# The last group of layer 2: a plain weight quadrant for the left-over block, its rows stored per two batches, and casts and sums in another order

## The chip, the cores and the metric

One core of one Trainium2 chip runs one launch of the kernel. The metric is the device time of that launch in microseconds (us). TensorE does the matrix products, VectorE (DVE) the element-wise work on two operands, ScalarE (ACT) casts, copies and activations, and SyncE (SP) issues most of the transfers; each engine takes its own instructions strictly in program order and waits on semaphores for the others. Transfers issued by SP and by ACT run on 16 shared DMA engines.

## What is computed

The reference is linear attention over 4 batches of 576 rows, followed by two feed-forward layers; only the second layer is touched:

```python
x = attention(q, k, v, omega)            # [4 * 576, 512]
r = np.maximum(x @ moe_w_in, 0.0);  x = (r * r) @ moe_w_out
h = x @ moe2_w_in                        # 512 -> 2048
g = np.where(h > 0.0, h, np.exp(np.minimum(h, 0.0)) - 1.0)
out = (g @ moe2_w_out).astype(np.float32)   # 2048 -> 512
```

## The kernel before

**Precision.** Every float32 operand is split into a high part (a cast on ACT, names ending in `h`) and a low part (a subtraction on DVE, recorded at line 77, names ending in `l`). A product is the sum of three matmuls: high by high, high by low, low by high.

**Tours.** The 2048 hidden columns of a layer are taken in four groups of 512. Within a group the rows come in five tours: four full ones (512 rows of one batch each, i = 0 to 3) and a left-over one, "block B", which holds the last 64 rows of all four batches (256 rows). In the last group of layer 2, written `(1, NG - 1)`, block B is the last tour of the kernel.

**Products by quadrants.** In the groups of the list `SECOND`, to which the last group of layer 2 belongs, both matrix products of a full tour use seven block products in place of eight. Each is 12 matmuls of 256 columns. In the first matrix product the seven operands of x are called b, t3, t2, p, t1, t4, q; they are read back from DRAM by SP (line 729), always five operands ahead of use in program order. In the second the hidden blocks "11", "12", "21", "22" and their differences t1 to t4 meet weight quadrants "A", "B", "C", "D" (function `strassen`, line 837). "A" is the pair of plain quadrants of the even weight slices; "B" holds the first plain quadrant of the odd slices beside the SUM of two second quadrants, since `make_floats` overwrites `b2` (line 172). The seven products are `p1` to `p7` in `quadrants`; they run one tour late, woven by `toured` (`earlier(0)` to `earlier(3)`) between the products of the next tour. Their results stand in PSUM banks x, r, y, z, v: bank y is copied by ACT to z in `p6` (line 880) and to v in `p7` (line 888), and p4 goes on in v. `grown` (line 921) adds a bank to the output rows in SBUF, in instructions of 256 columns on DVE, and in the last group at once calls `stored`, which issues the transfer to DRAM.

**Activation of layer 2.** `squares` gives three ACT instructions (relu, exp, tanh; four with a copy for block "12"), `joined` two on DVE (lines 951, 952), `difference` one on DVE (line 957), and `halved` a cast on ACT (line 963) and a subtraction on DVE.

**Order.** All of it is emitted in a hand-written order (`tc.manual_schedule()`): the place of a call in `toured` is its place in the queue of its engine. The list `carried` runs in the next tour after its first two products, `behind` after `earlier(0)` and `earlier(1)`, `sums` wherever `run(sums)` stands. Weight casts and their low parts are "chores", dealt out by `slot`.

**The left-over block** uses four products, in the order x += A by 11, x += B by 21 (`e0`), r += B by 21, r += A by d, with d = 11 - 21 (`e1`). Its output of 128 rows (two batches by 64) and 256 columns is stored by two transfers of 64 rows, one from SP and one from ACT (line 975); there are eight of these.

Of the kernel before, what the change touches and what calls it, by code (L numbers as in the profile page):

```python
# [17 lines left out]
def linear_attention_two_ffn_kernel(  # L18
# [12 lines left out]
    nc = tc.nc  # L31
# [115 lines left out]
    def make_floats(n):  # L147
        p = parts[n]
        t, m = staged.pop(p)
        nc.vector.scalar_tensor_tensor(  # L150
            out=t, in0=m.bitcast(U32), scalar=3, in1=t, op0=ALU.logical_shift_left, op1=ALU.bitwise_or
        )
        staged[p] = t.bitcast(F32)
        moe, f, o = p
        if not summed_up(p):
            return
        tf_t[f] = staged[p]
        names = "ABCD" if o else "abcd"
        if f % 2 == 0:
            casts.append(((moe, f, names[0]), tf_t[f]))  # L160
            return
        a, b = tf_t.pop(f - 1), tf_t.pop(f)
        sub = page([W], f"cs{moe}_{f}_{o}")
        if f % GF == 1:
            combos[f // GF] = page([W], f"cd{moe}_{f}_{o}")
        d = combos[f // GF][:, f % GF // 2 * HN:(f % GF // 2 + 1) * HN]
        (a1, a2), (b1, b2) = ((t[:, :HN], t[:, HN:]) for t in (a, b))
        s2, s3 = sub[:, :HN], sub[:, HN:]
        tt = nc.vector.tensor_tensor
        if o:  # L170
            tt(out=s3, in0=b1, in1=b2, op=ALU.subtract)
            tt(out=b2, in0=a2, in1=b2, op=ALU.add)
            tt(out=s2, in0=b2, in1=b1, op=ALU.subtract)
            tt(out=d, in0=a1, in1=s2, op=ALU.subtract)
        else:
            tt(out=s3, in0=a1, in1=b1, op=ALU.subtract)
            tt(out=b1, in0=b1, in1=b2, op=ALU.add)
            tt(out=s2, in0=b1, in1=a1, op=ALU.subtract)
            tt(out=d, in0=a2, in1=s2, op=ALU.subtract)
        casts.append(((moe, f - 1, names[1]), b))  # L180
        casts.append(((moe, f - 1, names[2]), sub))
        if f % GF == GF - 1:
            casts.append(((moe, f // GF * GF, names[3]), combos.pop(f // GF)))
# [642 lines left out]
    def strassen(tour, y, name, half, key, fresh):  # L826

        moe, g, k, i = tour
        gh, gl = g2_t[tour, key]
        for pr in range(2):  # L830
            wh, wl = ws_t[moe, g * GF + (0 if name == "D" else 2 * pr), name]
            c0 = pr * HN if name == "D" else half * HN
            for e in range(2):
                cs = slice(c0 + e * P, c0 + (e + 1) * P)
                ts = slice(pr * HN + e * P, pr * HN + (e + 1) * P)
                for m, (a, w) in enumerate(((gh, wh), (gh, wl), (gl, wh))):
                    nc.tensor.matmul(
                        y[:, e * HN:(e + 1) * HN],
                        *((a[:, ts], w[:, c0:c0 + HN]) if moe else (w[:, cs], a[:, pr * HN:(pr + 1) * HN])),
                        start=fresh and pr == 0 and e == 0 and m == 0, stop=pr == 1 and m == 2, skip_group_check=True,  # L840
                    )
# [7 lines left out]
    def quadrants(tour):  # L849

        moe, g, k, i = tour
        if moe == 0:
            sown(4, moe, g)
        elif k == 0 and (moe, g - 1) not in SECOND:
            del seeds[2:]
        nm = f"{moe}_{g}_{i}"
        bank = dict(zip("yzv", seeds[1:]))

        def part(to, name, half, key, fresh=False):
            if fresh:  # L860
                bank[to] = psum(f"p{to}{nm}")
            strassen(tour, bank[to], name, half, key, fresh)

        def add(to, l, u, last=True):
            sums.append(lambda: grown(tour, bank[to], l, u, last))

        def p1():
            part("x", "B", 0, "22", True)
            nc.scalar.copy(out=bank["y"], in_=bank["x"])

        def p5():
            part("r", "B", 1, "t1", True)
            add("r", 0, 0, False)
            add("r", 0, 1, False)

        def p6():
            part("y", "C", 0, "t2")
            sown(4, moe, g)
            bank.update(zip("zv", seeds[2:]))
            nc.scalar.copy(out=bank["z"], in_=bank["y"])  # L880

        def p2():
            part("x", "A", 0, "12")
            add("x", 1, 0)

        def p7():
            part("y", "C", 1, "t3")
            nc.scalar.copy(out=bank["v"], in_=bank["y"])
            add("y", 0, 1)

        def p3():
            part("z", "D", 0, "11")
            add("z", 0, 0)

        def p4():
            part("v", "A", 1, "t4")
            add("v", 1, 1)
            ended(tour)

        def e0():  # L900
            part("x", "A", 0, "11", True)
            part("x", "B", 0, "21")
            add("x", 0, 0)

        def e1():
            part("r", "B", 1, "21", True)
            part("r", "A", 1, "d")
            add("r", 0, 1)
            ended(tour)

        if i == B:
            return [[e0], [], [e1], []]
        return [[p1], [p5, p6], [p2, p7], [p3, p4]] if moe else [[p1, p5], [p6, p2], [p7, p3], [p4]]

    def grown(tour, y, l, u, last):
        moe, g, k, i = tour
# [50 lines left out]
    def stored(i, t, ya, cs):  # L967
        if i < B:
            (nc.scalar if (i, t) == (B - 1, 3) else nc.sync).dma_start(
                out=out[i * S:i * S + C * P, cs].rearrange("(p c) e -> p c e", c=C)[:, t, :], in_=ya[:, cs]  # L970
            )
            return
        for v in range(P // L):
            bb = t * (P // L) + v
            (nc.scalar if v else nc.sync).dma_start(out=out[bb * S + C * P:(bb + 1) * S, cs], in_=ya[v * L:(v + 1) * L, cs])

    def summed(tour, l):
        moe, g, k, i = tour
# [38 lines left out]
    def toured(before):  # L1017
# [3 lines left out]
        for n, tour in enumerate(tours):  # L1021
# [10 lines left out]
            if i == B:  # L1032
                bank_e, bank_o = psum(f"pe{nm}"), psum(f"po{nm}")
                times(tour, bank_e, "a", 0, "u", True, False, True)
                times(tour, bank_e, "a", 1, "v", False, True, False)
                read(tour, "v")
                run(carried)
                chores = chores_of(tour)
                slot(chores, 2)
                earlier(0)  # L1040
                carry(0)
                act = squares if second else act_a
                act(tour, "11", bank_e)
                times(tour, bank_o, "b", 0, "u", True, False, True)
                times(tour, bank_o, "b", 1, "d", False, True, False)
                read(tour, "d")
                earlier(1)
                carry(1)
                act(tour, "21", bank_o)
                joined()  # L1050
                if second:
                    halved(tour, "11")
                else:
                    act_b(tour, "11")
                run(sums)
                earlier(2)
                if second:
                    halved(tour, "21")
                    difference(tour, "d", "11", "21")
                    halved(tour, "d")  # L1060
                else:
                    act_b(tour, "21")
                slot(chores, 1)
                earlier(3)
                run(sums)
                if second:
                    todo = quadrants(tour)
                else:
                    todo = [[lambda tour=tour: chunk(tour, "11", True, False)], [], [lambda tour=tour: chunk(tour, "21", False, True)], []]
                continue  # L1070
# [30 lines left out]
            product(w, "b", 1, "t4")  # L1101
            nc.vector.tensor_tensor(out=c21, in0=w, in1=us, op=ALU.add)
            run(sums)
            act(tour, "22", c22)
            joined()
            slot(chores, 2)
            earlier(2)
            act(tour, "21", c21)
            joined()
            if second:  # L1110
                halved(tour, "22")
            else:
                act_b(tour, "22")
            product(b, "d", 0, "q")
            act(tour, "12", b)
            if second:
                run(sums)
                difference(tour, "t1", "21", "22")
                difference(tour, "t2", "11", "t1")
                halved(tour, "t1")  # L1120
                difference(tour, "t3", "11", "21", "21")
                joined()
            else:
                act_b(tour, "21")
            slot(chores, 1)
            earlier(3)
            run(sums)
            if second:
                carried.append(lambda tour=tour: halved(tour, "t2"))
                carried.append(lambda tour=tour: halved(tour, "12"))  # L1130
# [118 lines left out]
```

## Time and profile before

| | us |
|---|---|
| median of 3 runs (907.88 to 908.86) | 908.32 |
| the profiled execution, its own time | 908.27 |
| its span | 906.5 |
| PE busy | 894.5 |
| DVE busy | 711.2 |
| ACT busy | 607.7 |

The span runs from the first to the last instruction of the profile; 1.77 us of the execution's time lie outside it. PE is the matmul row; its instructions overlap, so that a stall is read from the distance of two starts, not from the busy share. The granted clock is at its full level in all 40 slices of the page.

### The profile page before, as it was taken

The numbers are of one execution on the slowest core, as the hardware profiler recorded it, in microseconds if no ns is written. First come the engines' busy times: TensorE is split into PE (matmuls) and PEld (weight loads), VectorE is DVE, ScalarE is ACT, GpSimd is POOL, SyncE is SP. The second block draws the span as 40 slices with busy tenths as digits, with TensorE's granted clock in tenths as the row PEclk, the third lists the DMA queues.
The fourth block names the chain that finished last, engine by engine and source line by source line (L and its number), as shares of the span: only waits on it lengthen the run. The fifth ranks groups of instructions, "written<-read, shape, count | busy, mean of one in ns | idle before, by whom it ended". The sixth has DMA issues, their size and how long they took to land. (4 is left out here: it accounts for less than half of the span.)

```text
span 906.5 us, 20710 instructions
## 1 busy us (share of the span) xinstructions
PE 894.5 (99%) x7807; PEld 844.4 (93%) x7807; DVE 711.2 (78%) x1329; ACT 607.7 (67%) x1292; POOL 86.8 (10%) x188
## 2 busy tenths in 40 slices
PE   8999999999999999999999999999999999999997
PEld 7888999998999999999999999899899989989997
DVE  5898875688876888777879897966597748878887
ACT  7999976664767675766366666755485638666663
POOL 4678730000000000000000000000000000000000
PEclk9999999999999999999999999999999999999999
DMA  9675522524998676577589664275468655653653
GB/s 242 168 196 159 170 83 75 177 94 154 349 374 302 216 250 239 179 231 255 197 279 335 244 209 164 96 256 195 160 203 270 222 183 168 205 200 126 222 173 94
DMA packets 134724, 183.89 MB, mean 203 GB/s; under 512 B 34272, under 2 KB 70624, under 8 KB 134624
## 3 DMA queue, kind: packets, MB, share of 16 engines
q1 hardware_dynamic: 133328, 181.88, 60.3%
q8 instruction: 62, 1.02, 0.5%
q10 hardware_dynamic: 1296, 0.69, 0.3%
q14 instruction: 38, 0.31, 0.1%
HBM read 145.29 MB, written 37.22 MB: 201 GB/s over the span
## 5 line engine op out<-in xcount | busy, mean ns | idle before, releaser
L810 PE MATMUL py<-wh,gh 128*128 128x512 f32 x216 | 85.2, 394 | 0.0
L810 PE MATMUL py<-wl,gh 128*128 128x512 f32 x216 | 85.1, 394 | 0.0
L810 PE MATMUL py<-wh,gl 128*128 128x512 f32 x216 | 85.1, 394 | 0.0
L782 DVE SCALAR_TENSOR_TENSOR r<-r,t 128x512 f32<-128x512 f32 x54 | 37.1, 687 | 57.4 <-ACT t L781 57.4
L77 DVE TENSOR_TENSOR gl<-gf,gh 128x512 fp32r<-128x512 f32 (+1 forms) x104 | 65.0, 625 | 4.1 <-ACT gh L792 0.5
L810 PEld LDWEIGHTS py<-wh,gl 128*128 128x128 f32 x216 | 40.6, 188 | 9.6
L810 PEld LDWEIGHTS py<-wl,gh 128*128 128x128 f32 x216 | 40.6, 188 | 7.4
L810 PEld LDWEIGHTS py<-wh,gh 128*128 128x128 f32 x216 | 40.6, 188 | 7.4
L135 ACT ACTIVATE cm<-st 128x512 f32<-128x512 f32 x64 | 44.2, 698 | 2.1 <-DMA st<-in_moe_w_out_dram 1.8
L792 ACT CAST gh<-gf 128x512 fp32r<-128x512 f32 x54 | 33.3, 617 | 17.0 <-DVE gf L783 16.1
L150 DVE SCALAR_TENSOR_TENSOR cv<-cm,cv 128x512 uint32<-128x512 uint32 x64 | 43.4, 685 | 0.8
L1082 ACT COPY pb<-pa 128x512 f32<-128x512 f32 x28 | 16.1, 574 | 40.1 <-PE pa L759 39.9
L1097 DVE TENSOR_TENSOR c<-pb,vs 128x512 f32<-128x512 f32 x28 | 19.3, 690 | 28.3 <-PE pb L759 21.7
L818 PE MATMUL py<-gh,wh 128*128 128x256 f32 x144 | 40.4, 281 | 0.0
L818 PE MATMUL py<-gh,wl 128*128 128x256 f32 x144 | 40.4, 281 | 0.0
L818 PE MATMUL py<-gl,wh 128*128 128x256 f32 x144 | 40.4, 281 | 0.0
L1090 ACT COPY us<-pb 128x512 f32<-128x512 f32 x28 | 16.4, 587 | 34.6 <-PE pb L759 29.1
L549 PE MATMUL ph<-xh,wh 128*128 128x256 f32 (+1 forms) x128 | 38.8, 303 | 0.0
L585 PE MATMUL py<-gh,wh 128*128 128x256 f32 (+1 forms) x128 | 38.4, 300 | 0.0
L585 PE MATMUL py<-gl,wh 128*128 128x256 f32 (+1 forms) x128 | 37.8, 295 | 0.0
L585 PE MATMUL py<-gh,wl 128*128 128x256 f32 (+1 forms) x128 | 37.8, 295 | 0.0
L549 PE MATMUL ph<-xh,wl 128*128 128x256 f32 (+1 forms) x128 | 37.7, 295 | 0.0
(1250 smaller groups left out, 3608.7 us busy)
## 6 DMA issues: line engine op xcount, KB each, us to landing
st<-in_moe_w_in_dram SPq DMA_DIRECT2D x32, 512.0 KB, 5.4
st<-in_moe_w_out_dram SPq DMA_DIRECT2D x32, 512.0 KB, 3.8
vk<-in_v_dram SPq DMA_DIRECT2D x32, 128.0 KB, 4.7
out_dram<-ya SPq DMA_DIRECT2D x30, 128.0 KB, 2.0
ld0k<-in_k_dram SPq DMA_DIRECT2D x4, 256.0 KB, 5.1
ld0q<-in_q_dram SPq DMA_DIRECT2D x4, 256.0 KB, 4.7
ld1k<-in_k_dram SPq DMA_DIRECT2D x4, 256.0 KB, 5.0
ld1q<-in_q_dram SPq DMA_DIRECT2D x4, 256.0 KB, 4.6
```

Source lines behind the costliest of these rows:

```text
L77: eng.tensor_tensor(out=out, in0=whole, in1=hi.bitcast(F32), op=ALU.subtract)
L135: nc.scalar.activation(out=staged[p][1], in_=staged[p][0][:, :, 1].bitcast(F32), func=AF.Prelu, scale=REBIAS, alpha=NEGATIVE)
L150: nc.vector.scalar_tensor_tensor(out=t, in0=m.bitcast(U32), scalar=3, in1=t, op0=ALU.logical_shift_left, op1=ALU.bitwise_or)
L549: nc.tensor.matmul(ph[:, :n], wt[:, cs], x_part(xt, i, c)[:, n0:n1], start=(m == 0), stop=(m == 3 * KD - 1))
L585: nc.tensor.matmul(y, w[:, ts], a, start=j == 0 and m == 0 and t % per == 0, stop=j == GF - 1 and m == 2, skip_group_check=per > 1,)
L782: nc.vector.scalar_tensor_tensor(out=r, in0=r, scalar=1.0, in1=t, op0=ALU.add, op1=ALU.mult)
L792: nc.scalar.copy(out=gh, in_=gf)
L810: nc.tensor.matmul(y_t[l, u], a[:, s0], w, start=first and pr == 0 and m == 0, stop=last and pr == 1 and m == 2,)
L818: nc.tensor.matmul(y_t[l, u][:, e * HN:(e + 1) * HN], w[:, ts], a[:, pr * HN:(pr + 1) * HN], start=first and pr == 0 and m == 0 and e == 0 ...
L1082: nc.scalar.copy(out=b, in_=a)
L1090: nc.scalar.copy(out=us, in_=b)
L1097: nc.vector.tensor_tensor(out=c22, in0=b, in1=vs, op=ALU.add)
```

## The change

Five edits, all for the last group of layer 2. (1) While the weights of that group are made, the plain second quadrant of each odd slice is copied to a further page "E" before it is overwritten, and "E" is split like the others. (2) The left-over block then computes r = A by 11 + E by 21, without the difference d; its four products come in the order x A 11, r A 11, x B 21, r E 21, each followed by its sums. (3) In `stored`, one transfer takes the rows of two batches, from SP for one half and from ACT for the other. (4) In full tours p7 stands ahead of p2; both stand ahead of the activation of "21", all three differences follow at once, the cast of t1 moves into the next tour (`carried`), and the sums of y and x move behind the activation of "12". (5) In the left-over tour the join of "11" moves ahead of the products of bank o, its cast and the sums of r ahead of p7 and p2, and these two ahead of the activation of "21"; the join and the cast of "21" follow, then the sums of y and x. In the diff the `else` branch that only repeats the old lines for other groups is cut.

```diff
@@ make_floats
+        if (moe, f // GF, o) == (1, NG - 1, 1):
+            e = combos["e"] = combos["e"] if "e" in combos else page([W], f"ce{moe}_{f}")
+            nc.vector.tensor_copy(out=e[:, f % GF // 2 * HN:(f % GF // 2 + 1) * HN], in_=b2)
+            if f % GF == GF - 1:
+                casts.append(((moe, f // GF * GF, "E"), combos.pop("e")))
@@ strassen
-            wh, wl = ws_t[moe, g * GF + (0 if name == "D" else 2 * pr), name]
-            c0 = pr * HN if name == "D" else half * HN
+            wh, wl = ws_t[moe, g * GF + (0 if name in "DE" else 2 * pr), name]
+            c0 = pr * HN if name in "DE" else half * HN
@@ quadrants
+        if (moe, g, i) == (1, NG - 1, B):
+            return [
+                [lambda: part("x", "A", 0, "11", True), lambda: part("r", "A", 1, "11", True)],
+                [lambda: part("x", "B", 0, "21"), lambda: add("x", 0, 0), lambda: part("r", "E", 0, "21"), lambda: add("r", 0, 1)],
+            ]
-        return [[p1], [p5, p6], [p2, p7], [p3, p4]] if moe else ...
+        return [[p1], [p5, p6], [p7, p2], [p3, p4]] if moe else ...
@@ stored
-        for v in range(P // L):
-            bb = t * (P // L) + v
-            (nc.scalar if v else nc.sync).dma_start(out=out[bb * S + C * P:(bb + 1) * S, cs], in_=ya[v * L:(v + 1) * L, cs])
+        n = P // L
+        (nc.scalar if t else nc.sync).dma_start(
+            out=out.rearrange("(b s) e -> b s e", s=S)[t * n:(t + 1) * n, C * P:, cs], in_=ya[:, cs]
+        )
@@ toured, left-over tour
                 act(tour, "11", bank_e)
+                if second and (moe, g) == (1, NG - 1):
+                    joined()
...
                 earlier(1)
+                if second and (moe, g) == (1, NG - 1):
+                    halved(tour, "11")
                 carry(1)
+                if second and (moe, g) == (1, NG - 1):
+                    run(sums)
+                    earlier(2)
                 act(tour, "21", bank_o)
...
@@ toured, full tour
+            if moe and second:
+                act(tour, "22", c22)
+                joined()
+                earlier(2)
+                act(tour, "21", c21)
+                joined()
                 halved(tour, "22")
                 difference(tour, "t1", "21", "22")
                 difference(tour, "t2", "11", "t1")
-                halved(tour, "t1")
                 difference(tour, "t3", "11", "21", "21")
+                product(b, "d", 0, "q")
+                act(tour, "12", b)
+                slot(chores, 2)
                 joined()
+                run(sums)
+                slot(chores, 1)
+                earlier(3)
+                run(sums)
+                carried.append(lambda tour=tour: halved(tour, "t1"))
...
```

## Rows read from the trace of the kernel before

**Rows 1.** The page: busy us, share of the span, instructions.
```profile
PE 894.5 (99%) x7807; PEld 844.4 (93%) x7807; DVE 711.2 (78%) x1329; ACT 607.7 (67%) x1292; POOL 86.8 (10%) x188
```
**Rows 2.** Busy time by stretches: stretch, us, each engine's busy us (instructions), clock, DMA.
```profile
858.00:900.00 42.00, 41.56 (x350) 41.16 (x349) 36.77 (x73) 25.59 (x47) 0.00 (x0) 1.00 0.35 120
```
**Rows 3.** Timeline of PE around the product with t4: start us, us, instruction [idle].
```profile
848.92 0.28 PE L759 MATMUL pb<-xst1h,wl_14b 128*128 128x256 f32 x1
850.02 0.39 PE L759 MATMUL pw<-xst4l,wh_12b 128*128 128x256 f32 x1 [0.31 <-DMA xst4l<-xd12t]
851.30 0.28 PE L759 MATMUL pw<-xst4h,wl_14b 128*128 128x256 f32 x1
...
869.71 0.28 PE L759 MATMUL pb<-xst1h,wl_14b 128*128 128x256 f32 x1
871.67 0.28 PE L759 MATMUL pw<-xst4h,wl_14b 128*128 128x256 f32 x1
```
**Rows 4.** Timeline of SP's queue ahead of the load of t4.
```profile
843.56 1.79 SPq L969 DMA_DIRECT2D out_dram<-ya  x4
845.45 0.40 SPq L729 DMA_DIRECT2D xst4h<-xd12t  x1
```
**Rows 5.** Timeline of ACT in the tour before that.
```profile
832.40 0.61 ACT L940 ACTIVATE t<-g 128x512 f32<-128x512 f32 x1
833.60 0.57 ACT L888 COPY pb<-pb 128x512 f32<-128x512 f32 x1 [0.59 <-PE pb L837]
```
**Rows 6.** Timeline of DVE in the same tour.
```profile
835.94 0.69 DVE L951 SCALAR_TENSOR_TENSOR r<-r,t 128x512 f32<-128x512 f32 x1 [0.67 <-ACT t L940]
...
840.58 0.69 DVE L77 TENSOR_TENSOR glt<-gt,ght 128x512 fp32r<-128x512 f32 x1
...
843.12 1.41 DVE L921 TENSOR_TENSOR ya<-pb,ya 128x256 f32<-128x256 f32 x4
```
**Rows 7.** Timeline of PE at the end.
```profile
892.93 0.28 PE L837 MATMUL pb<-wh_12D,gl 128*128 128x256 f32 x1
893.39 0.39 PE L837 MATMUL pb<-wh_12A,ght 128*128 128x256 f32 x1 [0.19 <-ACT pb L888]
...
894.79 0.28 PE L837 MATMUL pb<-wh_14A,glt 128*128 128x256 f32 x1
...
900.46 0.28 PE L837 MATMUL pr<-wh_14A,gld 128*128 128x256 f32 x1
```
**Rows 8.** Chain of waits that ended last: start us, us, what.
```profile
896.76 0.63 ACT ghd L963
...
898.11 2.98 DVE ya L921 x9
...
901.42 0.66 DVE ya L921 x2
```
**Rows 9.** Line 975: its issues on SP's queue (ns min/median/max, first and last start).
```profile
L975 SPq DMA_DIRECT2D out_dram<-ya x4: 546/550/580, 901.5 to 903.5; - x4
```
**Rows 10.** DMA from 830 to 907 us: packets, MB, share; issues, KB, landing us.
```profile
q10 hardware_dynamic: 608, 0.52, 2.4%
...
out_dram<-ya ACTq DMA_DIRECT2D x2, 128.0 KB, 2.0
out_dram<-ya ACTq DMA_DIRECT2D x4, 64.0 KB, 2.1
```
**Rows 11.** DMA from 843 to 845.4 us, in which four stores run alone.
```profile
q1 hardware_dynamic: 293, 0.27, 33.9%
```
**Rows 12.** DVE groups by form, 775 to 817 us: busy us, mean ns | idle before.
```profile
L951 DVE SCALAR_TENSOR_TENSOR r<-r,t 128x512 f32<-128x512 f32 x3 | 2.1, 686 | 3.1 <-ACT t L940 3.1
L77 DVE TENSOR_TENSOR wl_14A<-cv,wh_14A 128x512 fp32r<-128x512 f32 x1 | 0.7, 685 | 0.0
L172 DVE TENSOR_TENSOR cv<-cv,cv 128x256 f32<-128x256 f32 x1 | 0.4, 425 | 0.0
```

More of the change, by code (lines that the diff above doesn't have):

```diff
@@ L909, in e1 @@
             ended(tour)
+        if (moe, g, i) == (1, NG - 1, B):
[3 more added lines that the diff above has]
+            ]
         if i == B:
             return [[e0], [], [e1], []]
-        return [[p1], [p5, p6], [p2, p7], [p3, p4]] if moe else [[p1, p5], [p6, p2], [p7, p3], [p4]]
+        return [[p1], [p5, p6], [p7, p2], [p3, p4]] if moe else [[p1, p5], [p6, p2], [p7, p3], [p4]]
     def grown(tour, y, l, u, last):
@@ L1047, in toured @@
                 earlier(1)
+                if second and (moe, g) == (1, NG - 1):
+                    halved(tour, "11")
                 carry(1)
+                if second and (moe, g) == (1, NG - 1):
+                    run(sums)
+                    earlier(2)
                 act(tour, "21", bank_o)
-                joined()
-                if second:
+                if second and (moe, g) == (1, NG - 1):
+                    pass
+                    joined()
+                    halved(tour, "21")
+                elif second:
+                    joined()
                     halved(tour, "11")
@@ L1056, in toured @@
                 earlier(2)
-                if second:
+                if second and (moe, g) != (1, NG - 1):
                     halved(tour, "21")
@@ L1060, in toured @@
                     halved(tour, "d")
-                else:
+                elif not second:
                     act_b(tour, "21")
@@ L1103, in toured @@
             run(sums)
[L1104 to L1110, printed above, removed]
-                halved(tour, "22")
[L1112 to L1117, printed above, removed]
+            if moe and second:
+                act(tour, "22", c22)
+                joined()
+                earlier(2)
+                act(tour, "21", c21)
+                joined()
+                halved(tour, "22")
                 difference(tour, "t1", "21", "22")
                 difference(tour, "t2", "11", "t1")
-                halved(tour, "t1")
                 difference(tour, "t3", "11", "21", "21")
+                product(b, "d", 0, "q")
+                act(tour, "12", b)
+                slot(chores, 2)
                 joined()
-            else:
[L1124 to L1127, printed above, removed]
+                run(sums)
[3 more added lines that the diff above has]
+                carried.append(lambda tour=tour: halved(tour, "t1"))
+            else:
+                act(tour, "22", c22)
+                joined()
+                slot(chores, 2)
+                earlier(2)
+                act(tour, "21", c21)
+                joined()
+                if second:
+                    halved(tour, "22")
+                else:
+                    act_b(tour, "22")
+                product(b, "d", 0, "q")
+                act(tour, "12", b)
+                if second:
+                    run(sums)
+                    difference(tour, "t1", "21", "22")
+                    difference(tour, "t2", "11", "t1")
+                    halved(tour, "t1")
+                    difference(tour, "t3", "11", "21", "21")
+                    joined()
+                else:
+                    act_b(tour, "21")
+                slot(chores, 1)
+                earlier(3)
+                run(sums)
             if second:
```

## The prediction

> **What bounds the kernel now.** I read the page's busy line first: PE is busy in 99% of the span, the other engines in 78% and less [rows 1]. The reader is to see that an edit on DVE or ACT gains only where PE waits for it, or behind PE's last matmul. Then the stretch that the edits touch, from 858 us: PE 41.56 of 42 us, DVE 36.77, ACT 25.59 [rows 2]. So next PE's timeline, for starts further apart than usual. A product is 12 matmuls. From 894.79 to 900.46 there are four products without a stall [rows 7], 5.67 us, so that from the last start of one product to the last start of the next 1.42 us should pass. Three places miss that. Around the product with t4 of the tour i = 2 it is 851.30 - 848.92 = 2.38, a loss of 0.96, and the row names the load of t4; for i = 3 it is 871.67 - 869.71 = 1.96, a loss of 0.54 [rows 3]. At p4 of the last tour it is 894.79 - 892.93 = 1.86, a loss of 0.44, and the row names the copy to bank v (line 888) [rows 7]. Last, the chain of waits: it ends in the cast of d on ACT, eleven sums on DVE up to 902.08, and then only transfers [rows 8]: the last matmul starts at 900.46, the last of the eight small stores is issued at 903.5 and lands 2.1 later, at 905.6 [rows 7, 9, 10]; the span ends 0.9 later. The tail of 6 us behind PE and 1.9 us of stalls are all that the edits can save.
>
> **The change part by part.** All sums are made against the profiled execution (908.27: the span of 906.5 and 1.77 around it; the median is 908.32, 0.05 more).
>
> *The quadrant E.* Added are two DVE copies of 128 by 256, one ACT cast and one DVE subtraction. The copy is not in the trace; a DVE instruction of that size takes 0.425, the subtraction 0.685 [rows 12], the cast about the 0.61 of an ACT instruction of 128 by 512 [rows 5]: 0.85 + 0.69 + 0.61 = 2.15 us at most, and at least nothing. I take nothing: they fall into the stretch from 775 to 817 us, where DVE sat idle for 3.1 us ahead of three joins [rows 12], and no PE stall is near. With that cover gone it would be 2.15. Removed are the difference d, its cast and its subtraction (0.69 + 0.63 + 0.69), which stand in the chain [rows 8]. PE's count stays at four products.
>
> *p7 ahead of p2.* ACT's copy to v waits for p7: it starts at 833.60, 0.59 idle behind the tanh that began at 832.40 [rows 5]. One product earlier, p7 has ended when that tanh does (833.0), so that the copy and the activation of "21" start 0.6 earlier; the join of "21" on DVE, which waited 0.67 for it [rows 6], does too. In the last tour the copy's source ends 1.4 earlier, and the cast that stood ahead of it on ACT is gone from there: the 0.44 at p4 goes. Late next is the low part of t4, by my count 0.5 ahead of its use. Bounds 0 and 0.44; I take 0.44.
>
> *Sums behind the join of "12".* DVE's order between the join of "21" and the sums of z and v loses the subtraction of t1 (0.60 of queue time [rows 6]). So those sums, at 843.12 before [rows 6], end 0.65 + 0.6 = 1.25 earlier, at about 843.2; the sums of y and x now stand directly ahead of them, from 840.5. Queued behind on SP are the stores: eight in a row from 840.95. A store takes 0.45 of SP (four in 1.79 [rows 4]), so the last leaves by 844.7, SP being the limit, and not DVE. Behind them in SP's queue is the load of t4, which PE waits for: it leaves at 844.75 and not at 845.45 [rows 4], 0.7 earlier. That takes 0.7 of the 0.96 for i = 2. For i = 3 I get 1.6 earlier by the same count, which covers the 0.54 whole. Sum 1.2; bounds: nothing (eight stores back to back slow the load by what it gains) and 1.5. The cast of t1, moved into the next tour, is due at p5, seven products in; its low part is ready 1 us before. p1's low weights (14B) come earlier on DVE than before.
>
> *The end of the left-over block, if a transfer behaves as now.* PE's last matmul starts at 900.0 and ends at 900.3. DVE: the subtraction of "21" ends at 896.8 (the activation of "21" ends at 894.2, then two instructions to join, a cast, a subtraction, 0.65 each), 0.5 before PE needs it, since its product is now the third of four. Eight sums at 0.331 (2.98 for nine [rows 8]) end at 899.45, the two of x at 900.1, the two of r at 901.0 (902.08 before). The stores were eight, four to a queue, 0.55 each [rows 9]; now four, two to a queue: the last is issued at 901.1 and not at 903.5. That is 2.4 earlier, the 0.44 included.
>
> *The transfer itself.* On the side of DRAM its outermost step now has a count of two (the batches), then 64 rows; in SBUF it has 128 partitions. The trace has no such transfer. What it has: ACT's queue made 608 packets for two stores of 128 rows and four of 64 [rows 10], and 2 x (128 + 16) + 4 x (64 + 16) = 608. So each row of 1 KB is a packet, and each transfer has 16 closing ones, one for each engine, at 64 rows as at 128. Both counts cut evenly into 16. Two bounds follow. Above in speed: the store is spread over 16 engines and lands after 2.0, as the 128 KB stores do [rows 10]. Below: a transfer is cut along the outermost step of both sides, and two cuts into two only. Then each of two engines takes 64 packets, and if the four stores have the same two engines, 256. A packet took 0.339 x 16 x 2.4 / 293 = 0.044 [rows 11], or 0.024 x 16 x 77 / 512 = 0.058 with the closing ones counted in [rows 10]; I take 0.05. The first of the four is issued at 900.0 (the first sum of x ends 0.41 after 899.45); with 1.8 of fixed time (2.1 less 4 packets of 0.058 [rows 10]) the last lands at 900.0 + 1.8 + 256 x 0.05 = 914.6. The nearest row by size is the fast end. I take the slow one nevertheless, because the rows differ from this transfer in just the point that decides: their outermost counts are 64 and 128 on both sides, and nothing in the trace shows the address pattern regrouped ahead of the engines.
>
> The Trainium skill speaks against this edit. "DMA: Bandwidth & Descriptors", section "Why a DMA increments its semaphore by 16 and not by 1", has the number of engines as the largest up to 16 that divides the slowest dimension of both sides, and on this queue the lowest-numbered ones. By that rule the slow end holds; the 16 closing packets at 64 and 128 rows agree with it, and no run so far shows a count of two.
>
> The forecast: 908.27 + (914.6 - 905.6) - 1.2 = 916.1, some 7.8 slower.
>
> **The rivals.**
>
> *Spread over 16 engines* (the other side: faster). Then 908.27 - 2.4 - 1.2 = 904.7. For it: every transfer in the trace is spread so. Against it: none has a small outermost count. It decides from 16 closing packets per store at line 975.
>
> *Two engines, but not the same two for all four.* With a pair for each queue an engine has 128 packets: 900.0 + 1.8 + 6.4 = 908.2, which gives 908.27 + 2.6 - 1.2 = 909.7; with a pair for each transfer the last lands at 901.1 + 1.8 + 3.2 = 906.1 and it is 907.6. Nothing in the rows bears on it.
>
> *Spread over 16, but PE waits for bank x.* The sums of x now end at 841.8 (from 840.5, four at 0.33), and p1 of the next tour, which writes a bank x anew, began at 840.49 by its place in PE's queue. If the new x lies in the old one's bank, PE waits 1.3 there, 0.5 and 0.8 in the next two tours: 904.7 + 2.6 = 907.3. For it: eight banks are all taken. Against it: the bank of r is free by then as well.
>
> **How the numbers follow.** Two engines and the same ones: 0.69. 16 engines: 0.21. Two engines in other pairs: 0.05. The wait for bank x with 16 engines: 0.05. The predicted time is that of the first. Its own range: with 0.044 a packet and all of 1.5 from t4 it is 914.3; with 0.058 and nothing from t4 919.3; two engines alone may be faster than sixteen together, which no row shows, and a quarter under 0.05 is 912.6. So 912.5 to 919.5. That alone holds less than 8 in 10, and the likeliest other case lies on the other side, so the range reaches to the 16 engines with a little more gain than I count: 904.2 to 919.5. A difference under 0.2% (1.8 us) can't be told from none; faster (under 906.5) has 0.21, no change (906.5 to 910.1) 0.08 from the last two cases, slower 0.71.
>
> **What would show it.** Right: at line 975 four transfers whose landing times climb from about 5 to 13 us, two closing packets for each, and a DMA share near 2/16 after 902 us while all engines are idle. Right in the small terms: the starts around t4's product 1.43 to 1.7 apart, none of 0.44 lost at p4, the last matmul 1.6 earlier, no difference d in the chain. Wrong: landings of 2 us at line 975 (then 904.7); a wait of px on DVE's sums; PE stalls at E's product, which would mean that the casts are not covered.

## The result, and the profile after

The changed kernel takes 916.84 us (median of 4 runs, 916.09 to 917.79) against 908.18 (4 runs, 907.88 to 908.86) of the kernel before beside it: the ratio is 1.0092, with an interval of 1.0079 to 1.0105. It is slower, by 8.7 us where 7.8 were forecast. The profiled execution took 916.74, its span is 914.9.

The page, busy line and (its section on queues) the queue of ACT:

```profile
PE 894.5 (98%) x7807; PEld 844.3 (92%) x7807; DVE 711.0 (78%) x1330; ACT 607.3 (66%) x1292; POOL 86.7 (9%) x188
...
q10 hardware_dynamic: 1236, 0.69, 0.2%
```

The same queue on the page of the kernel before:

```profile
q10 hardware_dynamic: 1296, 0.69, 0.3%
```

PE does the same work in the same time [rows 1]. The queue's line decides the question of the transfer. Outside the left-over block the queue has 976 packets in both kernels: the kernel before has 1296 on its page, less 4 x (64 + 16). Here 260 are left for two transfers of 128 rows: 2 x (128 + 2). A merged transfer has two closing packets and not 16.

The issues of the four merged transfers (ns min/median/max, first and last start), and busy time by stretches: stretch, us, each engine's busy us, clock, DMA share, GB/s:

```profile
L984 SPq DMA_DIRECT2D out_dram<-ya x2: 539/596/652, 900.0 to 901.4; - x2
L984 ACTq DMA_DIRECT2D out_dram<-ya x2: 547/869/1191, 900.3 to 901.7; - x2
```

```profile
858.00:900.00 42.00, 41.12 (x344) 40.61 (x343) 35.23 (x72) 23.85 (x43) 0.00 (x0) 1.00 0.39 130
902.00:904.00 2.00, 0.00 (x0) 0.00 (x0) 0.00 (x0) 0.00 (x0) 0.00 (x0) 0.77 0.13 31
904.00:906.00 2.00, 0.00 (x0) 0.00 (x0) 0.00 (x0) 0.00 (x0) 0.00 (x0) 0.50 0.13 38
906.00:908.00 2.00, 0.00 (x0) 0.00 (x0) 0.00 (x0) 0.00 (x0) 0.00 (x0) 0.50 0.14 48
910.00:912.00 2.00, 0.00 (x0) 0.00 (x0) 0.00 (x0) 0.00 (x0) 0.00 (x0) 0.50 0.14 48
912.00:914.00 2.00, 0.00 (x0) 0.00 (x0) 0.00 (x0) 0.00 (x0) 0.00 (x0) 0.50 0.10 36
```

The last store is issued at 901.7, 1.8 earlier than before [rows 9]. Then every engine is idle, and the DMA share stands at 0.13 to 0.14, about two engines of 16, until the data run out: 36 of 48 GB/s in the last stretch is 1.5 of its 2 us, so at 913.5. These two engines move 31 and 38 GB/s up to 906 and 48 from then on. 48 GB/s on two engines are 24 GB/s each, 0.043 us for a packet of 1 KB.

PE's timeline around the product with t4 and in the last tour (start us, us, instruction, idle before it), to be held against [rows 3, 7]:

```profile
848.85 0.28 PE L764 MATMUL pb<-xst1h,wl_14b 128*128 128x256 f32 x1
849.47 0.38 PE L764 MATMUL pw<-xst4l,wh_12b 128*128 128x256 f32 x1 [0.23 <-DMA xst4l<-xd12t]
850.76 0.28 PE L764 MATMUL pw<-xst4h,wl_14b 128*128 128x256 f32 x1
...
869.23 0.28 PE L764 MATMUL pb<-xst1h,wl_14b 128*128 128x256 f32 x1
870.02 0.39 PE L764 MATMUL pw<-xst4l,wh_12b 128*128 128x256 f32 x1 [0.22 <-DMA xst4l<-xd13t]
871.32 0.28 PE L764 MATMUL pw<-xst4h,wl_14b 128*128 128x256 f32 x1
...
888.32 0.28 PE L842 MATMUL pb<-wh_14C,glt 128*128 128x256 f32 x1
889.26 0.39 PE L842 MATMUL pb<-wh_12C,ght 128*128 128x256 f32 x1 [0.66 <-ACT pb L885]
890.66 0.28 PE L842 MATMUL pb<-wh_14C,glt 128*128 128x256 f32 x1
893.49 0.28 PE L842 MATMUL pb<-wh_12D,gl 128*128 128x256 f32 x1
894.91 0.28 PE L842 MATMUL pb<-wh_14A,glt 128*128 128x256 f32 x1
900.61 0.28 PE L842 MATMUL pr<-wh_12E,gl 128*128 128x256 f32 x1
```

Less 1.42 for a product, 0.49 and 0.67 are lost at t4 (0.96 and 0.54 before). The stall at p4 is gone: 894.91 - 893.49 = 1.42. In its place stands a new one: p7 now follows p6 directly, writes on in bank y, and waits for ACT's copy of y to z (line 885): 890.66 - 888.32 is 2.34, a loss of 0.92. In the other tours two products of the next tour stand between p6 and p7; in the last there are none.

SP's queue in the tours i = 2 and 3, and DVE at the end:

```profile
840.90 3.77 SPq L979 DMA_DIRECT2D out_dram<-ya  x8
844.76 0.40 SPq L734 DMA_DIRECT2D xst4h<-xd12t  x1
```

```profile
860.73 5.00 SPq L979 DMA_DIRECT2D out_dram<-ya  x8
865.83 0.39 SPq L734 DMA_DIRECT2D xst4h<-xd13t  x1
```

```profile
896.05 0.69 DVE L77 TENSOR_TENSOR gl<-g,gh 128x512 fp32r<-128x512 f32 x1 [0.69 <-ACT gh L973]
...
899.51 0.76 DVE L931 TENSOR_TENSOR ya<-px,ya 128x256 f32<-128x256 f32 x2
900.93 0.76 DVE L931 TENSOR_TENSOR ya<-pr,ya 128x256 f32<-128x256 f32 x2 [0.66 <-PE pr L842]
```

The eight stores stand back to back and the load of t4 leaves at 844.76 [rows 4]. DVE's last sums now follow PE's last product directly; no difference d is in the chain [rows 8].

### The profile page after: what moved, and what is told of

The parts are those of the page before. It is cut to its first block, busy times and chain, and to the rows that moved or that the text cites. A ratio compares the mean times of both kernels' runs of the same rounds, so it can differ in the third digit from the quotient of the medians.

```text
span 914.9 us, 20706 instructions
## 1 busy us (share of the span) xinstructions
PE 894.5 (98%) x7807; PEld 844.3 (92%) x7807; DVE 711.0 (78%) x1330; ACT 607.3 (66%) x1292; POOL 86.7 (9%) x188
## 4 chain that ended last, share of the span: by engine, by line
PE 86%; DVE 4%; ACT 4%; DMA 2%; issue 1%; SPq 0%; POOL 0%; DVEq 0%; ACTq 0%; POOLq 0%
PE py L815 16%; PE pb L764 12%; PE pa L764 8%; PE pw L764 8%; PE pb L842 6%; PE py L823 5%; PE ph L554 5%; PE py L590 5%; PE px L842 4%; PE pr L842 2%; PE po L764 2%; PE pe L764 2%; PE pn L442 1%; PE px L474 1%; DVE ya L936 1%
```

## Experiments

Theory T: the two cuts of the merged transfers cost what the kernel lost, and the rest of the change gains a little. Rivals: R1, the merged transfers cost nothing and the order or the quadrant E does; R2, it is the size or the issue of the transfers, not their outermost count. Ratios are to the kernel before, run beside it on the same chip.

| kernel | us | before | ratio, 95% interval |
|---|---|---|---|
| changed kernel | 916.84 | 908.18 | 1.0092 [1.0079, 1.0105] |
| e1: eight stores of 64 rows back | 907.02 | 908.85 | 0.9978 [0.9969, 0.9987] |
| e2: before, merged stores only | 918.99 | 908.85 | 1.0110 [1.0094, 1.0125] |
| e3: two of four merged | 912.01 | 908.85 | 1.0033 [1.0021, 1.0045] |
| e4: before, stores of 34 and 30 rows | 913.63 | 908.75 | 1.0052 [1.0039, 1.0066] |
| e5: before, stores of 32 rows | 910.13 | 908.75 | 1.0017 [1.0008, 1.0026] |
| e6: e1, p2 ahead of p7 in the last tour | 906.85 | 908.85 | 0.9976 [0.9967, 0.9984] |
| e7: e6, loads six ahead | 905.98 | 908.75 | 0.9969 [0.9956, 0.9981] |
| e8: before, quadrant E only | 908.30 | 908.75 | 0.9994 [0.9985, 1.0003] |
| e9: e7, whole rows stored | 906.14 | 909.05 | 0.9965 [0.9952, 0.9977] |
| e10: before, loads six ahead | 906.90 | 909.05 | 0.9979 [0.9970, 0.9989] |

**The transfer: e1, e2, e3.** The edit undone (e1, the diff), done alone on the kernel before (e2, the diff reversed), and done by half (e3 merges SP's half and leaves the other as four stores of 64 rows):

```diff
-        n = P // L
-        (nc.scalar if t else nc.sync).dma_start(
-            out=out.rearrange("(b s) e -> b s e", s=S)[t * n:(t + 1) * n, C * P:, cs], in_=ya[:, cs]
-        )
+        for v in range(P // L):
+            bb = t * (P // L) + v
+            (nc.scalar if v else nc.sync).dma_start(out=out[bb * S + C * P:(bb + 1) * S, cs], in_=ya[v * L:(v + 1) * L, cs])
```

> The changed kernel with its eight stores of 64 rows back, all else as changed. Theory 1 (a transfer with an outermost count of two runs on two engines, and that alone makes the kernel slow): the sums end as in the changed kernel, the last store is issued near 902.0 and lands 2.1 later, the span ends near 905.0 and the time is about 906.8, 0.15% under the kernel before. Theory 2 (the new order, with PE's wait of 0.94 for the copy of bank y, makes it slow): over 912.

> The kernel before with the merged stores alone. Theory 1: the first of four is issued near 901.2, 256 packets follow at 0.043 us on each of two engines, the last lands near 914, the time is about 916.6. Theory 2: no slower than before (908.2), or 1 us faster since four issues fall away.

> The changed kernel, but only the half that SP stores is merged (two transfers), the other half goes in four stores of 64 rows. Theory 1 (all merged transfers share the same two engines): 128 packets on each of them in place of 256, data from 901.3 to 906.8, the time about 910.0 (909 to 911). If each merged transfer is slow by itself and they do not share: as the changed kernel, 916; with a pair of engines for each transfer: about 907.

All three go the way of T, but only e1 meets its size. e2 lies 2.4 above its expected time and e3 1.0 above its range; 0.7 of either is the kernel before, which took 908.85 there and not 908.18. In e2 the first merged store is issued at 902.0 and not at 901.2, and its two engines move only 28 and 38 GB/s from 904 to 908, as in the changed kernel at first; for e3 the excess was not taken apart. With none, two and four transfers merged the ratio is 0.9978, 1.0033, 1.0092: 5.0 and 5.4 us for each pair, where 128 packets at 0.043 are 5.5. R1 falls with e1 and e2 together: without the merged stores the change gains about 2 us, with nothing but them the kernel before loses 10.1. e3 shows on the way that transfers queue on the same engines. Its issues and landing times (KB each, median us to landing):

```profile
out_dram<-ya ACTq DMA_DIRECT2D x2, 64.0 KB, 4.9
out_dram<-ya SPq DMA_DIRECT2D x2, 64.0 KB, 6.1
```

These are the plain stores of the other half. Before, those of ACT landed after 2.1 [rows 10] and those of SP after 2.0; behind two merged ones they take 4.9 and 6.1.

**The count alone: e4, e5.** Each store of 64 rows is cut in two, once where neither part divides by 16, once in the middle:

```diff
-            (nc.scalar if v else nc.sync).dma_start(out=out[bb * S + C * P:(bb + 1) * S, cs], in_=ya[v * L:(v + 1) * L, cs])
+            for r0, r1 in ((0, 34), (34, L)):      # e5: ((0, 32), (32, L))
+                (nc.scalar if v else nc.sync).dma_start(
+                    out=out[bb * S + C * P + r0:bb * S + C * P + r1, cs], in_=ya[v * L + r0:v * L + r1, cs]
+                )
```

> The kernel before with each of its eight stores of 64 rows cut in 34 and 30 rows of one batch: no step from batch to batch is in any transfer. Theory 1 (the rows are shared out evenly over as many engines as divide both outermost counts, up to 16): 34 rows run on 2 engines and 30 on 15, closing packets 2 and 15 in place of 16 and 16; the first two engines get 8 x 17 + 8 x 2 = 152 packets of 0.043 us, data to about 909.1, the time about 912.3, 2 us over the cut in 32 and 32. Rival (the merged store was slow for its long step in DRAM between two batches): 16 closing packets or near it, and the same time as the cut in 32 and 32.

> The control for the cut in 34 and 30: 32 and 32 rows, also sixteen transfers. 16 engines for each by theory 1; each queue issues eight at 0.55 us, the last near 905.4, the time about 910.3.

The queue of ACT on the pages of e4 and e5:

```profile
q10 hardware_dynamic: 1300, 0.69, 0.3%
```

```profile
q10 hardware_dynamic: 1360, 0.69, 0.3%
```

Less the 976, e4 has 324 = 4 x (34 + 2) + 4 x (30 + 15) and e5 has 384 = 8 x (32 + 16). The count itself gives 16 for 32 rows and 17 for each pair of 34 and 30 rows, which 2 and 15 make up. The same bytes in the same number of transfers cost 4.9 us in e4 and 1.4 in e5: R2 falls, and 3.5 us hang on the count. Only 2 were expected: e5 came out 0.2 under its expected time, e4 1.3 over, and why is open. By the Trainium skill ("DMA: Bandwidth & Descriptors", section "Why a DMA increments its semaphore by 16 and not by 1") the engines are the largest number up to 16 that divides the slowest dimension of both sides; the 2 closing packets at a count of 2 beside 128, the 16 at 32 and the 17 at 34 and 30 together agree with it. In the stretches of e4 the DMA share falls towards that of two engines at the end, as in the changed kernel, but it is sooner over:

```profile
906.00:908.00 2.00, 0.00 (x0) 0.00 (x0) 0.00 (x0) 0.00 (x0) 0.00 (x0) 0.50 0.30 88
908.00:910.00 2.00, 0.00 (x0) 0.00 (x0) 0.00 (x0) 0.00 (x0) 0.00 (x0) 0.50 0.18 58
```

**The new stall of p7: e6.**

```diff
+        if (moe, g, i) == (1, NG - 1, B - 1):
+            return [[p1], [p5, p6], [p2, p7], [p3, p4]]
         return [[p1], [p5, p6], [p7, p2], [p3, p4]] if moe else ...
```

> As the run with the 64-row stores back, and in the last tour p2 stands ahead of p7 again, so that p7 does not follow p6 directly on bank y. If the wait of p7 for the copy to z (0.94 between two starts in the changed kernel, 0.83 more than the usual pitch, and 0.1 behind it) is on the path that ends last: 0.9 under that run, about 905.9. If DVE and the stores end last anyway: no more than 0.2 under it. If the old stall at p4 comes back: 0.4 to 0.5 under it.

No wait is left in PE's last tour, yet the time moves by 0.2, less than the interval. This execution lost 1.06 at t4 and e1's lost 0.39, so the two traces can't be held against each other to a tenth, and what the stall of 0.92 costs in time is not shown. What they agree on: DVE's last sum starts at 900.35 in both, behind PE in e1 and behind its own sums in e6:

```profile
900.35 0.76 DVE L931 TENSOR_TENSOR ya<-pr,ya 128x256 f32<-128x256 f32 x2 [0.66 <-PE pr L842]
```

```profile
899.68 0.75 DVE L933 TENSOR_TENSOR ya<-px,ya 128x256 f32<-128x256 f32 x2
900.35 0.76 DVE L933 TENSOR_TENSOR ya<-pr,ya 128x256 f32<-128x256 f32 x2
```

**The wait for t4: e7, e10.** The operands of x are loaded six ahead, so that the load of t4 stands ahead of the stores in SP's queue:

```diff
-    XA = 5
+    XA = 6
```

> As the run with 64-row stores and p2 ahead of p7 in the last tour, with the operands of x read six ahead in place of five, so that the load of t4 stands in SP's queue ahead of the previous tour's stores. If PE's losses around the product with t4 (0.5 and 0.7 in the changed kernel) come from the stores ahead of the load: both gone, 0.7 to 1.2 under that run. If they come from full pages or from the DMA engines: no change, or slower by other loads that wait for a page.

> The kernel before, with x's operands loaded six ahead in place of five and nothing else. It tests the prediction's term of t4 alone: PE lost 0.96 and 0.54 us waiting for the load of t4 behind the stores in SP's queue. If those are on the path to the end, 1.5 of loss goes and the time is 1.0 to 1.5 under the kernel before, some 907.4 on a base of 908.7. Rival: the loss is given back at p4 of the last tour or in the DVE tail (what PE gains, DVE's sums do not follow), so that it is within 0.3 of the kernel before. A second rival: the loads put earlier wait for pages that come free late, and it is slower by up to 1.

In both the stalls at t4 are gone: PE's waits from 775 us on are none in e7 and the one at p4 in e10 (what waits, for what: us in total, times, longest):

```profile
PE pb L837 <- ACT pb L888: 0.2, 1, 0.2
```

e10 gains 2.15, with an interval of 1.0 to 2.7, where 1.0 to 1.5 were expected. The other traces fit the higher value: the loss at t4 is not the 1.50 of one execution. The five with the old order (before, e2, e4, e5, e8) lost 1.50, 2.04, 1.69, 2.43 and 2.03, 1.94 on average; the four with the new order (changed, e1, e3, e6) 1.16, 0.39, 0.47 and 1.06, 0.77 on average. e7 stands 2.77 under its kernel before and e6 2.00, near the low end of the 0.7 to 1.2 that were expected, but their intervals overlap, so that this gain is not shown.

**The quadrant alone: e8** (edits 1 and 2 of the change on the kernel before, and the difference d gone, the order otherwise as before; of the diff only what is not in the change's own).

```diff
-                    difference(tour, "d", "11", "21")
-                    halved(tour, "d")
+                    if (moe, g) != (1, NG - 1):
+                        difference(tour, "d", "11", "21")
+                        halved(tour, "d")
```

> The kernel before with the quadrant E and its order of the four products of the left-over block alone; stores of 64 rows, the full tours and the left-over tour's casts as before. If d in the chain and the order of the four products are most of what the other edits gain: the sums of r end near 901.5 (902.08 before), the last store is issued near 901.8 (903.5), the time 1.5 to 1.8 under the kernel before. If the orders of the tours make the gain: within 0.5 of before.

A miss: 0.45 less, within the interval of none. Behind PE's last matmul (901.30) the tail is 4.7 long, 1.3 shorter than before, as expected; but that matmul starts 0.84 later than before. 0.53 of this is t4, which lost 2.03 in this execution. Most of the rest comes from the edit itself. PE waits once for the low part of the weight 14B:

```profile
820.56 0.28 PE L842 MATMUL px<-wh_14B,gh 128*128 128x256 f32 x1
821.14 0.39 PE L842 MATMUL px<-wl_14B,gh 128*128 128x256 f32 x1 [0.31 <-DVE wl_14B L77]
...
821.71 0.28 PE L842 MATMUL px<-wh_14B,gl 128*128 128x256 f32 x1
```

These six matmuls take 1.15 from first start to last, where five steps of 0.12 would be 0.60: 0.55 is lost. The first of them starts 0.33 earlier than in the kernel before (820.89), so that 0.55 - 0.33 + 0.53 = 0.75 of the 0.84 is accounted for. On DVE the subtraction for E (0.6 of its queue) stands ahead of that for 14B, with no idle time left between them. No such wait is in the changed kernel: there the subtraction of t1, which edit 4 moves to the next tour, is gone from that place.

**Whole rows: e9.**

```diff
+        if cs.start == 0:
+            return
...
-            (nc.scalar if v else nc.sync).dma_start(out=out[bb * S + C * P:(bb + 1) * S, cs], in_=ya[v * L:(v + 1) * L, cs])
+            (nc.scalar if v else nc.sync).dma_start(out=out[bb * S + C * P:(bb + 1) * S, :], in_=ya[v * L:(v + 1) * L, :])
```

> The kernel that loads six operands ahead, with the left-over block's output stored by four transfers of 64 whole rows (512 columns, 2 KB a row) in place of eight of 64 half rows, each issued once both halves are summed. Theory (issues of 0.55 us in two queues are what is left behind the last sums): in that kernel's trace the last of the eight is issued at about 901.2 with the last sum ending near 900.0; with two per queue, of which the first pair is issued when the first 128 rows are whole, the last leaves about 1.1 earlier, so 1.1 under it: 904.9 on the same base, and 16 closing packets for each transfer. Rival: a row of 2 KB takes longer to land than one of 1 KB, and the sums, not the issues, end last, so that the gain is 0.3 or less: 905.7 to 906.0. By the count of packets the transfer stays on 16 engines in either case, so a time above 908 speaks against both.

The last store is issued at 899.5 and not at 901.2, and nothing measurable comes of it (0.9965 against 0.9969), as the rival in the expectation had it. The rows of e9 show where a part of it went: a store of whole rows lands 2.4 to 3.0 after its issue, the smaller ones of e7 after 2.0 to 2.3:

```profile
L989 SPq DMA_DIRECT2D out_dram<-ya x2: 547/550/552, 898.8 to 899.5; - x2
L989 ACTq DMA_DIRECT2D out_dram<-ya x2: 567/688/808, 898.8 to 899.5; - x2
...
DMA to landing us min/median/max: 2.4/2.6/3.0
```

e7 and e9 are the fastest of all, 2.8 and 2.9 us under the kernel before.

## Why the prediction was right, and where its terms were not

- *The transfer itself*: right, and it decides. Two closing packets, two engines, and the same two for all four transfers (e3's late landings). The packet was mis-sized: 0.043 and not 0.05, which is 10.9 for 256 and not 12.8. The merged stores' landings are not in the trace; with the 0.9 that lay between the last landing and the end of the span before, the last one is at 914.0, 12.2 behind 900.0 and the fixed 1.8. So 0.6 of the 1.9 arrives. Most of the other 1.3 is in the first stretches: from 902 to 906 the two engines are as busy as later but move 31 and 38 GB/s in place of 48, 54 KB less, which is 1.1 us. In the trace 23 of the 512 packets take 0.07 to 0.26 us, the others 0.046, and all 23 start before 904.5. The stores of the full tours have ended at 901.2, so they are not what slows these packets; the cause is open.
- *Sums behind join 12*: the load of t4 left when the prediction said (844.76 against 844.75) in the tour i = 2. For i = 3 it left at 865.83, where it had left at 866.31 before: 0.48 earlier, not 1.6. The eight stores ahead of it took 5.00 us, of which 1.25 is the excess of one long issue (last section). Of 1.2 the profiled execution shows 0.34 (1.50 to 1.16). Over the nine executions of kernels with either order it is 1.94 - 0.77 = 1.17, the size predicted. What failed was to read a loss that varies between executions from one of them: 1.94 stood to be saved and not 1.50, and 0.77 is left and not 0.3, so that the difference came out right and its two ends did not.
- *p7 ahead of p2*: this step failed. The 0.44 at p4 went, as predicted, but the step asked only who waits for p7, not what p7 waits for: in the last tour it meets ACT's copy of bank y, and PE loses 0.92. That is outside the bounds of 0 and 0.44, on the other side. In the full tours PE has no such wait.
- *E quadrant*: the 0 taken is right for the changed kernel, which has no PE stall near it, but not for the reason given. The idle time of DVE did not cover the subtraction: in e8 it makes 14B late and PE loses 0.55. In the changed kernel the moved subtraction of t1 makes room for it.
- *The end, if a transfer behaves as now*: the last matmul starts at 900.61, where 900.0 less 1.2 was forecast, 1.8 later: 0.92 from p7 and 0.86 from t4. The first merged store is 1.2 later than forecast (900.0 against 898.8) and its transfer 0.6 shorter, which leaves the 0.6 between 916.74 and 916.1. That the whole is within 0.7 is in part luck: the transfer was taken 0.6 too long and the way to it 1.2 too short.
- *The rivals*: 16 engines falls with the two closing packets; without the merge the ratio is 0.9978 (e1), about 2 us of gain and not the 3.6 of that rival, which had four stores. Other pairs of engines fall with the DMA share of two engines for all four transfers, and with e3. There is no wait of PE for bank x in the trace.

Shown by runs: that the merged transfers cost it (e1 to e3) and that the count of the outermost step does (e4, e5). Argued from traces only: how the smaller terms add up. Edits 4 and 5 were not run by themselves.

## What to carry over

Before two small transfers are put into one, look at the outermost count that the new one has on both sides: here a count of 2, or 34, left most DMA engines idle, and at the end of this kernel nothing hid it. The closing packets in a queue's count on the page tell how many engines a transfer got. A product that is moved ahead must be checked for what it waits for in each tour, the last above all; and a stall worth a microsecond is priced from several executions, not one.

## What was not expected of the hardware

SP needed 3.77 us for eight stores in one tour and 5.00 in the next: one issue took 1.65 us, from 863.11, where the median was 0.40. Within that run of stores, between 862.5 and 863.2, the trace has a packet of the queue that carries instructions. In e1, e3 and e6 one issue in the same run of stores takes 1.01, 1.01 and 1.55, with such a packet within 0.4 us of its start. Whether that is the cause was not tried. Nor is it known why the loss at t4 varies from 1.50 to 2.43 with the same order.
